# A new order table, and planned times from a replay of five queues, in a FAVOR attention and softplus MLP kernel

## The chip, the cores and the metric

The kernel runs on one core of one Trainium2 chip. The metric is the device time of one execution in microseconds (us). Work is spread over TensorE (PE, matrix products), VectorE (DVE), ScalarE (ACT), GpSimd (POOL) and the DMA queue that SyncE (SP) issues. Each engine takes its own instructions strictly in the order in which the program emitted them; between engines there are only semaphores.

## The reference

```python
q, k, v: (8, 8, 576, 64)      omega: (128, 64)
def phi(x):                    # x scaled by 64 ** -0.25
    h = x @ omega.T - sum(x * x) / 2
    return exp(h - max(h)) / sqrt(128)
kv, z = phi(k).T @ v, sum(phi(k))
attn  = (phi(q) @ kv) / (phi(q) @ z + 1e-6)
x = attn as 4608 tokens x 512
h = x @ w_in                   # 512 -> 2048
g = max(h, 0) + log1p(exp(-abs(h)))
out = g @ w_out                # 2048 -> 512
```

All is float32. The kernel gets near it by splitting operands into a high part in TensorE's fast fp32r form and a low remainder, and by three products (high-high, high-low, low-high) where the reference has one.

## The kernel before, in words

**Tiling.** The 64 heads of 576 rows form 16 quads of four heads (names such as `_4_1_`: batch 4, second quad), each cut into units of 128 rows (`_5_0_2` is unit 2). Keys come first: `xk` is loaded, squared (L594) and summed (L599), split into `spk` high (a cast, L623) and low (a subtraction, L627), projected to `ppk` (L609 in the first batches, L634 later), added up (L647), reduced to a maximum (L651, L659), and exponentiated on ScalarE (L656); `s` sums features (L844, L847), `kt` and `kvs` hold the product with v. Queries go the same way, are multiplied with z for the denominator (`den`, L1006, a multiply with an accumulated sum), inverted (L1011), divided (L1015), turned (`flip`, L1040), written to DRAM and read back as `qq` (L1047, L1063), and multiplied with `kvs` into `xp` (L1096), which is split into `xh` and `xl` (L1110, L1116). In batch 0 the queries skip that turn: `nuq` (L935) is divided on VectorE into `xq` (L939 to L943) and turned by TensorE into `xfq` (L951).

**The MLP** takes tokens in blocks: two of 256 (worked on in turns), then 512 each; `h_5_2` is block 5, feature chunk 2 of 16. Twelve matmuls give `h` (L1167 to L1169), three ScalarE passes and one on VectorE give `u` (L1182), its cast is `gh` (L1186) and the remainder `gl` (L1190), and 12 matmuls add to `acc` (L1227 to L1229), copied out as `o` (L1239, L1244). The last two blocks (tokens from 3584 and 4096) share chunks in pairs: a Strassen-like scheme of seven products `pa`, `pb`, `pc` (L1501) on sums of weights (`tf`, L1423 to L1443, split into `t` and `wi`) and of tokens, collected by VectorE as `ha`, `hb`, `hc` (L1530 to L1539). In it, the fourth product goes into the bank `pb` that the seventh used, so it starts once `hc` (L1534) has read that bank.

**What sets the order.** A step is a `Work`: the engines that may do it with a cost each, what it comes `after`, the buffers that it takes and gives. The table `ORDER` lists every work once, as twice its number plus the choice of its engine. `in_order` (L341) goes through the table, gives each work the buffer that has been free longest by its planned time, and plans its start and end; nothing but the table and these buffers decides what is emitted, and engines follow the emission. `with_fill` (L376) then looks at the planned ends on TensorE and, where a planned gap is long enough, emits `fill` matmuls (L1683) that multiply the identity and whose result is not used. VectorE and GpSimd share an access to SBUF; the plan lets one of them have it at a time for works marked `port`, and in the planned times it goes to the works in the table's order.

The lines that decide this:

```python
e = list(w.on)[k % 2]
t = max([clock.get(e, 0.0)] + [x.end + x.delay for x in w.after])
shared = e == "POOL" or e == "DVE" and w.port
t = max(t, port if shared else 0.0)
n = int((t - last - (0.05 if t < 16 else 0.25)) / (0.43 if t < SLOW else 0.224))
```

Of the kernel before, what the change touches and what calls it, by code (L numbers as in the profile page):

```python
# [19 lines left out]
P = 128  # L20
S = 576
D = 64
M = 128
# [12 lines left out]
SLOW = 7.2  # L36
# [1754 lines left out]
```

## Time and profile before

| | |
|---|---|
| median of 3 runs | 1008.64 us (1008.28 to 1010.65) |
| the profiled execution | 1010.17 us, of which the span is 1008.2 us |
| TensorE busy (matmul) | 985.2 us, 98% |
| VectorE busy | 828.0 us, 82% |
| ScalarE busy | 711.8 us, 71% |
| GpSimd busy | 281.8 us, 28% |
| mean DMA rate | 113 GB/s, 340 and 405 GB/s in the first two of 40 slices |

The span runs from the first to the last instruction of the program; the time of the execution has 1.97 us more around it. A busy share is a mean over stages: a stage in which TensorE has idle time is limited by something else, and the engine that is busy nearly all of that stage is the first to look at.

### The profile page before, as it was taken

To read this page: it belongs to the slowest core of one execution; us is meant where nothing else is said; L and a number is where in the kernel's file an instruction comes from. 1 tells how busy PE (TensorE), PEld (TensorE's weight loads), DVE (VectorE), ACT (ScalarE), POOL (GpSimd) and SP (SyncE) were. 2 spreads that over 40 slices of the span, in tenths; PEclk is the share of its full clock that TensorE was granted. 3 is DMA by queue.
4 is the path that set the end of the run, shared out by engine and by line. 5 is a ranking of instruction groups with operands and counts; after the bars stand their busy time and mean duration, and the time that the engine had idled before them with its cause. 6 is when DMAs were issued, how large, how long until landed. Compare 5 with 4: busy or idle time off the path is not lost. (4 is left out here: it accounts for less than half of the span.)

```text
span 1008.2 us, 17087 instructions
## 1 busy us (share of the span) xinstructions
PE 985.2 (98%) x5563; PEld 809.0 (80%) x5563; DVE 828.0 (82%) x2147; ACT 711.8 (71%) x1735; POOL 281.8 (28%) x251
## 2 busy tenths in 40 slices
PE   8989999999999999999999999999999999999998
PEld 7878888788888888887778887877878778778886
DVE  6999988888888888878889988888888847998710
ACT  5999976668777786878687787878667635675700
POOL 2344432243334331325123441234122012121100
PEclk9999999999999999999999999999999999999999
DMA  9944644423452523441524333352422331000002
GB/s 340 405 144 139 203 128 129 136 76 100 128 153 85 160 80 123 142 131 56 151 83 128 98 118 108 108 148 89 125 95 80 103 96 43 1 1 1 1 11 73
DMA packets 64769, 113.82 MB, mean 113 GB/s; under 512 B 18316, under 2 KB 37672, under 8 KB 64680
## 3 DMA queue, kind: packets, MB, share of 16 engines
q1 hardware_dynamic: 64520, 112.60, 35.2%
q8 instruction: 44, 0.72, 0.3%
q14 instruction: 45, 0.37, 0.1%
q10 hardware_dynamic: 160, 0.13, 0.0%
HBM read 85.68 MB, written 27.03 MB: 112 GB/s over the span
## 5 line engine op out<-in xcount | busy, mean ns | idle before, releaser
L1227 PE MATMUL acc<-wo,gh 128*128 128x512 f32 x512 | 204.0, 398 | 1.6 <-ACT o L1244 1.2
L1228 PE MATMUL acc<-wo,gh 128*128 128x512 f32 x512 | 200.5, 392 | 0.0
L1229 PE MATMUL acc<-wo,gl 128*128 128x512 f32 x512 | 199.5, 390 | 0.0
L1167 PE MATMUL h<-xh,wi 128*128 128x512 f32 (+1 forms) x512 | 189.8, 371 | 2.4 <-DVE u L1182 2.2
L1168 PE MATMUL h<-xl,wi 128*128 128x512 f32 (+1 forms) x512 | 186.7, 365 | 0.3 <-DVE xl L968 0.3
L1169 PE MATMUL h<-xh,wi 128*128 128x512 f32 (+1 forms) x512 | 186.0, 363 | 0.0
L1190 POOL TENSOR_TENSOR gl<-u,gh 128x512 fp32r<-128x512 f32 (+1 forms) x71 | 86.2, 1214 | 227.3 <-ACT gh L1186 111.7
L1227 PEld LDWEIGHTS acc<-wo,gh 128*128 128x128 f32 x512 | 96.3, 188 | 26.2 <-issue 5.0
L1167 PEld LDWEIGHTS h<-xh,wi 128*128 128x128 f32 x512 | 96.7, 189 | 24.4 <-DVE u L1182 6.0
L1229 PEld LDWEIGHTS acc<-wo,gl 128*128 128x128 f32 x512 | 96.2, 188 | 20.9
L1169 PEld LDWEIGHTS h<-xh,wi 128*128 128x128 f32 x512 | 96.7, 189 | 15.7
L1228 PEld LDWEIGHTS acc<-wo,gh 128*128 128x128 f32 x512 | 96.5, 188 | 15.8
L1168 PEld LDWEIGHTS h<-xl,wi 128*128 128x128 f32 x512 | 96.8, 189 | 13.9 <-DVE xl L968 0.5
L1173 ACT ACTIVATE u<-h 128x512 f32<-128x512 f32 (+1 forms) x128 | 69.6, 544 | 46.9 <-PE h L1169 38.9
L1006 DVE CUSTOM_DVE_ANT_0 junk<-phq,zb 128x128 bf16<-128x128 f32 (+1 forms) x228 | 82.8, 363 | 10.8 <-ACT spk L623 0.2
L1182 DVE SCALAR_TENSOR_TENSOR u<-h,u 128x512 f32<-128x512 f32 (+1 forms) x128 | 78.2, 613 | 11.8 <-ACT u L1179 11.4
L1179 ACT ACTIVATE u<-u 128x512 f32<-128x512 f32 (+1 forms) x128 | 74.0, 579 | 2.5
L1176 ACT ACTIVATE u<-u 128x512 f32<-128x512 f32 (+1 forms) x128 | 73.8, 578 | 2.7
L656 ACT ACTIVATE phk<-phk,smk 128x128 f32<-128x128 f32 x208 | 67.0, 394 | 5.7 <-DVE smk L671 5.6
L656 ACT ACTIVATE phq<-phq,smq 128x128 f32<-128x128 f32 x194 | 61.3, 393 | 10.6 <-DVE smq L671 10.6
L1015 POOL TENSOR_TENSOR phq<-phq,dnq 128x512 f32<-128x512 f32 (+1 forms) x34 | 37.7, 1117 | 82.4 <-DVE dnq L1011 49.3
L1186 ACT CAST gh<-u 128x512 fp32r<-128x512 f32 (+1 forms) x83 | 45.6, 552 | 12.6 <-PE acc L1228 6.5
(220 smaller groups left out, 2004.2 us busy)
## 6 DMA issues: line engine op xcount, KB each, us to landing
xk<-kx SPq DMA_DIRECT2D x28, 512.0 KB, 3.5
xq<-qx SPq DMA_DIRECT2D x28, 512.0 KB, 3.5
fdq<-flq SPq DMA_DIRECT2D x28, 512.0 KB, 2.6
qq<-fdq SPq DMA_DIRECT2D x112, 128.0 KB, 3.5
rawi<-wi SPq DMA_DIRECT2D x16, 512.0 KB, 8.5
rawo<-wo SPq DMA_DIRECT2D x16, 512.0 KB, 9.9
out<-o SPq DMA_DIRECT2D x32, 256.0 KB, 3.5
v<-vv SPq DMA_DIRECT2D x14, 576.0 KB
```

The costliest lines, as they stand in the source:

```text
L656: nc.scalar.activation(x, x, AF.Exp, bias=b["sm"][:, 2, c : c + 1])
L1006: nc.vector.tensor_tensor_reduce(jk[r, c % jk.shape[1]], ph[r, c], q.zb[r, h], 1.0, 1e-6, ALU.mult, ALU.add, dn[r, 0, c : c + 1])
L1167: nc.tensor.matmul(b["h"], wh, xh[:, cc, t], start=cc == 0, stop=False)
L1168: nc.tensor.matmul(b["h"], wh, xl[:, cc, t], start=False, stop=False)
L1169: nc.tensor.matmul(b["h"], wl, xh[:, cc, t], start=False, stop=cc == NCC - 1)
L1176: nc.scalar.activation(b["u"], b["u"], AF.Exp, scale=-1.0)
L1179: nc.scalar.activation(b["u"], b["u"], AF.Ln, bias=1.0)
L1182: nc.vector.scalar_tensor_tensor(b["u"], b["h"], 0.0, b["u"], ALU.max, ALU.add)
L1190: (nc.vector if e == "DVE" else nc.gpsimd).tensor_tensor(b["gl"], b["u"], b["gh"].bitcast(F32), ALU.subtract)
L1227: nc.tensor.matmul(dst, gh, w2[fc][:, 0, c], start=start, stop=False, **kw)
L1228: nc.tensor.matmul(dst, gh, w2[fc][:, 1, c], start=False, stop=False, **kw)
L1229: nc.tensor.matmul(dst, gl, w2[fc][:, 0, c], start=False, stop=stop, **kw)
```

## The change

`ORDER` is replaced as a whole: the same works in another order, and for some of them the other engine. By engines, the program has 4837 instructions on TensorE before and 4832 after (the fills: 30 and 25, the five of the very start among them), 2149 and 2143 on VectorE, 1739 and 1712 on ScalarE, 256 and 289 on GpSimd, 453 and 453 on SyncE. GpSimd takes over low parts of `spq` (8), divisions (5), squares of `xq` (5), `gl` (4), `g` (4) and sums `s` (6) among others; VectorE gains 8 casts `gh`, 7 casts `spk` and 11 copies of `phk` and `phq` that ScalarE had, and gives up what went to GpSimd.

The planner gets a second pass, `timed`, which replays five queues: each engine's works in their order, the one that can start first going next, and the shared access going to whichever engine asks for it first. Its times replace those of `in_order` ahead of `with_fill`. Costs and delays in the plan change, and `plan_x` makes its two high parts ahead of its two low parts. Line numbers in the code past the table are 50 higher after than before.

```diff
-SLOW = 7.2
+SLOW = 7.9
+LULL, LULLED = 20.7, 0.9
 ORDER = (
-    384, 394, 386, 410, 434, 456, 415, 418, 440, 462, 437, 390, 392, 396, 398, 416, 400, 402, 478, 500, 522, 544, 388,
...
+    618, 542, 580, 560, 620, 562, 582, 656, 584, 586, 432, 598, 600, 654, 476, 690, 11, 60, 602, 604, 50, 622, 606,
...
-        self.delay = delay or (0.23 if "PE" in on else 0.19)
+        self.delay = delay or (0.21 if "PE" in on else 0.19 if "POOL" in on else 0.14)
...
         if shared:
-            port = w.end
+            port = w.end - (0.13 if e == "POOL" else 0.07)
...
+def timed(out, held):
+    queues = {e: [w for w in out if w.engine == e] for e in ("ACT", "DVE", "PE", "POOL", "SP")}
+    clock, head, ready, done = {e: START.get(e, 0.0) for e in queues}, dict.fromkeys(queues, 0), {}, set()
+    ports, mode, lull = {"DVE": -1.0, "POOL": -1.0}, None, LULLED
+    while len(done) < len(out):
+        best = None
+        for e, q in queues.items():
+            if head[e] == len(q):
+                continue
+            w = q[head[e]]
+            if e not in ready:
+                before = w.after + w.needs + (w.co.needs if w.co else [])
+                if any(id(x) not in done for x in before):
+                    continue
+                ready[e] = max([clock[e]] + [x.end + x.delay for x in before])
+            t = max(ready[e], ports["DVE"] if e == "POOL" else ports["POOL"] if e == "DVE" and w.port else 0.0)
+            if best is None or t < best[0] - 1e-9:
+                best = t, e, w
...
+        w.end = clock[e] = t + w.cost
+        if e == "POOL" or e == "DVE" and w.port:
+            ports[e] = w.end - (0.13 if e == "POOL" else 0.07)
...
-            "SP", dma(P * 4 * cols) + (0.7 if apart and q.qd else 0), load, behind=prev.get("load"),
+            "SP", dma(P * 4 * cols) + (1.6 if early and kind == "k" and u == 1 and not q.qd else 0), load, behind=prev.get("load"),
...
-                "DVE", 0.415 if u < 4 else 0.63, lambda c=c: den(c), after=es + [q.zc] if d is None else [d], behind=d,
+                "DVE", 0.34 if u < 4 else 0.64, lambda c=c: den(c), after=es + [q.zc] if d is None else [d], behind=d,
...
-            "DVE", dve(n * M), flip, after=done, give=[(bu, "phs")], take=[("flip", b, "vs")], port=True,
+            "DVE", dve(n * M), flip, after=done, give=[(bu, "phs")], take=[("flip", b, "vs")],
...
-            h = l = None
+            l = None
             for p in range(2):
-                h = do(
+                hs.append(do(
                     ("DVE", "ACT"), (dve(m) + extra, act(m, PSUM) + extra), lambda e, p=p: x_high(e, p),
-                    after=[a] + old_reads(t0, m), behind=h,
-                )
+                    after=[a] + old_reads(t0, m), behind=hs[-1] if hs else None,
+                ))
+            for p in range(2):
                 l = do(
-                    "DVE", dve(m), lambda p=p: x_low(p), after=[h], behind=l if one else None,
+                    "DVE", dve(m), lambda p=p: x_low(p), after=hs if one else [hs[p]], behind=l if one else None,
...
-        for w in with_fill(*in_order(works, room), room["any"], 1e9, fill):
+        out_, held = in_order(works, room)
+        timed(out_, held)
+        for w in with_fill(out_, held, room["any"], 1e9, fill):
```

**Place A, TensorE, the first queries of batch 0** (the two quads `0_0` and `0_1`; `nuq` numerators, `xfq` turns, `ppq` projections, `h_0_0` the first chunk of the MLP). Before:

```order
L935 MATMUL nuq_0_1_0_609<-kvs_0_1_563,xq_0_1_0_184 128x65 x4
L935 MATMUL nuq_0_1_1_617<-kvs_0_1_563,xq_0_1_1_273 128x65 x4
L935 MATMUL nuq_0_0_2_624<-kvs_0_0_461,xq_0_0_2_277 128x65 x4
L951 MATMUL xfq_0_1_0_630<-ident_72,xq_0_1_0_184 128x128 x2
L951 MATMUL xfq_0_1_1_641<-ident_72,xq_0_1_1_273 128x128 x2
L609 MATMUL ppq_0_1_3_0_648<-omf_82,xq_0_1_3_324 128x128
L609 MATMUL ppq_0_1_3_1_649<-omf_82,xq_0_1_3_324 128x128
```

After:

```order
L985 MATMUL nuq_0_1_0_605<-kvs_0_1_585,xq_0_1_0_209 128x65 x4
L985 MATMUL nuq_0_1_1_612<-kvs_0_1_585,xq_0_1_1_273 128x65 x4
L659 MATMUL ppq_0_1_3_0_620<-omf_82,xq_0_1_3_320 128x128
L659 MATMUL ppq_0_1_3_1_621<-omf_82,xq_0_1_3_320 128x128
L659 MATMUL ppq_0_1_3_0_620<-omf_82,xq_0_1_3_320 128x128
L659 MATMUL ppq_0_1_3_1_621<-omf_82,xq_0_1_3_320 128x128
L1001 MATMUL xfq_0_1_0_628<-ident_72,xq_0_1_0_209 128x128 x2
L1217 MATMUL h_0_0_645<-xh_79,wi0_312 128x256
```

`xfq_0_1_0` and `xfq_0_1_1` stood right behind the numerators; now the projections of unit 3 stand ahead of the first of them, and six matmuls of `h_0_0` and a numerator stand between the two.

**Place B, VectorE, where block 5 of the MLP begins** (`den` rows carry `junk`; their second rows read the sum; `o_4_1` is a copy of block 4's output; `u_5_0` frees the bank that `h_5_2` takes on TensorE). Before, the last rows ahead of `u_5_0`:

```order
L1006 ISA junk_78,dnq_5_0_0_1_6273<-phq_5_0_0_0_6143,zb_5_0_6228 128x128
L1006 ISA dnq_5_0_0_1_6273 128x1
L1006 ISA junk_78,dnq_5_0_0_0_6252<-phq_5_0_0_0_6143,zb_5_0_6228 128x128
L1006 ISA dnq_5_0_0_0_6252 128x1
L1011 RECIPROCAL dnq_5_0_0_1_6273<-dnq_5_0_0_1_6273 128x4
L671 SCALAR_TENSOR_TENSOR smk_5_1_0_5988<-smk_5_1_0_5988 128x8
L1239 COPY o_4_1_6296<-acc_4_1_5133 128x256
L1182 SCALAR_TENSOR_TENSOR u_5_0_6319<-h_5_0_6111,u_5_0_6319 128x512
```

After:

```order
L673 CAST spq_5_0_2_6268<-xq_5_0_2_6245 64x512
L1289 COPY o_4_0_6281<-acc_4_0_5117 128x256
L1056 ISA junk_78,dnq_5_0_0_1_6243<-phq_5_0_0_0_6104,zb_5_0_6218 128x128
L1056 ISA dnq_5_0_0_1_6243 128x1
L1056 ISA junk_78,dnq_5_0_0_1_6243<-phq_5_0_0_0_6104,zb_5_0_6218 128x128
L1056 ISA dnq_5_0_0_1_6243 128x1
L677 TENSOR_TENSOR spq_5_0_2_6268<-xq_5_0_2_6245,spq_5_0_2_6268 64x512 x2
L1232 SCALAR_TENSOR_TENSOR u_5_0_6311<-h_5_0_6198,u_5_0_6311 128x512
```

Three of the eight `den` pairs now come behind `u_5_0`, and the cast and the two low parts of `spq_5_0_2`, whose low parts GpSimd did before, come ahead of it. On TensorE, three matmuls of `acc_4_3` now stand between `h_5_1` and `h_5_2`, where nothing stood before.

**Place C, VectorE, chunk pair 4 of the last two blocks** (`tf` are sums of weights for pair 5). Before:

```order
L1530 TENSOR_TENSOR hb_4_10269<-pb_4_10248,ha_4_10235 128x512
L1308 SCALAR_TENSOR_TENSOR u_3584_7_10277<-hb_3_10127,u_3584_7_10277 128x512
L1428 TENSOR_TENSOR tf0_5_10263<-wi11_1508 128x256
L1429 TENSOR_TENSOR tf0_5_10263<-tf0_5_10263,tf1_5_10264 128x256
L1442 TENSOR_TENSOR tf2_5_10265<-wi10_1245,tf0_5_10263 128x256
L1443 TENSOR_TENSOR tf2_5_10265<-tf2_5_10265,wi10_1245 128x256
L1534 TENSOR_TENSOR hc_4_10294<-pb_4_10248,ha_4_10235 128x512
L1535 TENSOR_TENSOR hc_4_10294<-pc_4_10241,hc_4_10294 128x512
```

After:

```order
L1580 TENSOR_TENSOR hb_4_10265<-pb_4_10252,ha_4_10229 128x512
L1371 TENSOR_TENSOR g_4096_7_10242<-u_4096_7_10161,g_4096_7_10242 128x512
L1358 SCALAR_TENSOR_TENSOR u_3584_7_10240<-hb_3_10122,u_3584_7_10240 128x512
L1478 TENSOR_TENSOR tf0_5_10246<-wi11_1516 128x256
L1479 TENSOR_TENSOR tf0_5_10246<-tf0_5_10246,tf1_5_10247 128x256
L1584 TENSOR_TENSOR hc_4_10286<-pb_4_10252,ha_4_10229 128x512
L1585 TENSOR_TENSOR hc_4_10286<-pc_4_10208,hc_4_10286 128x512
L1492 TENSOR_TENSOR tf2_5_10248<-wi10_1254,tf0_5_10246 128x256
L1493 TENSOR_TENSOR tf2_5_10248<-tf2_5_10248,wi10_1254 128x256
```

The two `tf2_5` rows have gone behind both `hc_4` rows, and one `g` row has come in ahead of `u_3584_7`. For pair 2 the same rows stand as before, but the `u_4096_3` row that stood between `hb_2` and `hc_2` now stands ahead of `hb_2`.

## Rows read from the trace of the kernel before

**Rows 1.** The page: busy time of each engine, share of the span, instructions.

```profile
PE 985.2 (98%) x5563; PEld 809.0 (80%) x5563; DVE 828.0 (82%) x2147; ACT 711.8 (71%) x1735; POOL 281.8 (28%) x251
```

**Rows 2.** Windows: start:end, length, busy us by engine, granted clock, DMA share, GB/s.

```profile
0.00:50.00 50.00, 44.68 (x348) 39.54 (x349) 40.28 (x141) 37.52 (x110) 15.19 (x23) 0.97 0.98 373
50.00:125.00 75.00, 70.35 (x578) 59.40 (x578) 73.36 (x196) 71.11 (x193) 32.81 (x28) 1.00 0.50 161
125.00:475.00 350.00, 349.98 (x2015) 288.18 (x2015) 297.71 (x815) 261.84 (x663) 114.63 (x102) 1.00 0.39 118
475.00:525.00 50.00, 46.65 (x255) 36.80 (x254) 44.04 (x115) 36.42 (x89) 14.63 (x13) 1.00 0.36 107
525.00:850.00 325.00, 322.32 (x1700) 260.51 (x1699) 272.79 (x706) 231.51 (x548) 86.87 (x71) 1.00 0.35 105
850.00:925.00 75.00, 72.50 (x321) 59.24 (x320) 69.45 (x126) 47.63 (x91) 13.54 (x12) 1.00 0.01 4
36.00:44.00 8.00, 5.79 (x52) 4.96 (x50) 7.90 (x25) 6.18 (x17) 2.65 (x4) 1.00 1.03 409
45.00:48.00 3.00, 3.00 (x16) 2.55 (x15) 2.97 (x13) 2.48 (x8) 1.03 (x1) 0.50 1.03 410
```

**Rows 3.** Timeline at the start, TensorE and GpSimd: start, length, [idle before <-releaser].

```profile
12.30 2.88 PE L1683 MATMUL fill<-ident 128*128 128x128 f32 x16
...
12.58 0.61 POOL L594 TENSOR_TENSOR xk<-xk 128x256 f32<-128x256 f32 x1 [0.37 <-DMA xk<-k]
```

**Rows 4.** Timeline of TensorE at the first queries of batch 0.

```profile
42.75 0.41 PE L951 MATMUL xfq<-ident,xq 128*128 128x128 f32 x2 [0.77 <-DVE dnq L939]
43.49 0.41 PE L951 MATMUL xfq<-ident,xq 128*128 128x128 f32 x2 [0.33 <-DVE xq L943]
```

**Rows 5.** Timeline of SyncE's issues and TensorE at 478 to 486 us.

```profile
478.54 2.64 SPq L1063 DMA_DIRECT2D qq<-fdq  x4
...
485.18 1.08 PE L1096 MATMUL xp<-qq,kvs 128*64 128x256 f32 x8 [1.12 <-DMA qq<-fdq]
```

**Rows 6.** Timeline of GpSimd, VectorE and TensorE where block 5 begins.

```profile
513.76 2.73 POOL L627 TENSOR_TENSOR spq<-xq,spq 64x512 fp32r<-64x512 f32 x2 [4.99 <-ACT spq L623]
...
515.31 1.32 DVE L1006 CUSTOM_DVE_ANT_0 junk<-phq,zb 128x128 bf16<-128x128 f32 x1
516.57 0.08 DVE L1006 DVE_READ_ACCUMULATOR2_ANT dnq<- 128x1 f32 x1
516.68 0.29 DVE L1006 CUSTOM_DVE_ANT_0 junk<-phq,zb 128x128 bf16<-128x128 f32 x1
...
518.77 0.50 PE L1167 MATMUL h<-xh,wi 128*128 128x512 f32 x1 [1.01 <-DVE u L1182]
```

**Rows 7.** Timeline of VectorE, GpSimd and TensorE in chunk pairs 2 and 4.

```profile
871.81 0.68 DVE L1308 SCALAR_TENSOR_TENSOR u<-h,u 128x512 f32<-128x512 f32 x1
...
873.32 1.46 DVE L1442 TENSOR_TENSOR tf<-wi,tf 128x256 f32<-128x256 f32 x1
...
873.22 1.28 POOL L1321 TENSOR_TENSOR g<-u,g 128x512 fp32r<-128x512 f32 x1 [3.01 <-ACT g L1316]
...
875.89 0.50 PE L1501 MATMUL pb<-xh,t 128*128 128x512 f32 x1 [1.62 <-DVE hc L1534]
...
901.45 0.43 DVE L1442 TENSOR_TENSOR tf<-wi,tf 128x256 f32<-128x256 f32 x1
901.91 1.41 DVE L1443 TENSOR_TENSOR tf<-tf,wi 128x256 f32<-128x256 f32 x1
...
903.97 0.50 PE L1501 MATMUL pb<-xh,t 128*128 128x512 f32 x1 [0.60 <-DVE hc L1534]
```

**Rows 8.** Groups by line and shape: count, busy us, mean ns, idle before.

```profile
L1190 POOL TENSOR_TENSOR gl<-u,gh 128x512 fp32r<-128x512 f32 x50 | 66.2, 1324 | 174.7 <-ACT gh L1186 74.5 <-DVE gh L1186 51.1 <-DVE dnq L1011 15.1
...
L1006 DVE CUSTOM_DVE_ANT_0 junk<-phq,zb 128x128 bf16<-128x128 f32 x224 | 81.7, 365 | 10.7 <-ACT spk L623 0.2
...
L1190 DVE TENSOR_TENSOR gl<-u,gh 128x512 fp32r<-128x512 f32 x46 | 33.3, 726 | 2.8 <-ACT gh L1186 1.8
...
L1186 DVE CAST gh<-u 128x512 fp32r<-128x512 f32 x38 | 17.9, 471 | 2.5 <-PE acc L1228 0.7
```

More of the change, by code (lines that the diff above doesn't have):

```diff
@@ L319, with __init__ @@
 class Work:
-    def __init__(self, on, emit, after=(), take=(), give=(), delay=None, spare=0, behind=None, port=False, mode=None):
+    def __init__(self, on, emit, after=(), take=(), give=(), delay=None, spare=0, behind=None, port=False, mode=None, co=None):
         self.on, self.emit, self.port = on, emit, port
@@ L328, in __init__ @@
         self.take, self.give, self.spare = take, give, spare
-        self.delay = delay or (0.23 if "PE" in on else 0.19)
+        self.delay = delay or (0.21 if "PE" in on else 0.19 if "POOL" in on else 0.14)
         self.end, self.behind, self.engine = None, behind, None
         self.mode, self.cost = mode, 0.0
+        self.co, self.freed, self.needs = co, 0.0, []
 def change(old, new):
@@ L343, in in_order @@
     clock, held = dict(START), {}
-    free = {n: 0.0 for names in room.values() for n in names}
-    port, mode, out = 0.0, None, []
+    free = {n: (0.0, None) for names in room.values() for n in names}
+    port, mode, lull, out = 0.0, None, LULLED, []
     for k in ORDER:
@@ L353, in in_order @@
             assert len(names) > w.spare
-            box[key] = n = min(names, key=free.get)
-            t = max(t, free.pop(n))
+            box[key] = n = min(names, key=lambda n: free[n][0])
+            at, giver = free.pop(n)
+            w.freed = max(w.freed, at)
+            w.needs += [giver] if giver else []
             held.setdefault(n, []).append([t, 1e9, len(out), 1e9])
+        t = max(t, w.freed, w.co.freed if w.co else 0.0)
         shared = e == "POOL" or e == "DVE" and w.port
@@ L362, in in_order @@
         w.cost *= 2 if e == "PE" and t < SLOW else 1
+        if e == "SP" and t >= LULL:
+            w.cost, lull = w.cost + lull, 0.0
         w.end = clock[e] = t + w.cost
@@ L366, in in_order @@
         if shared:
-            port = w.end
+            port = w.end - (0.13 if e == "POOL" else 0.07)
         for box, key in w.give:
-            free[box[key]] = w.end + w.delay
+            free[box[key]] = w.end + w.delay, w
             held[box[key]][-1][1::2] = w.end + w.delay, len(out)
@@ L373, in in_order @@
     return out, held
+def timed(out, held):
[16 more added lines that the diff above has]
+                best = t, e, w
+            elif e == "POOL" and best[1] == "DVE" and t < best[0] + 1e-6 and best[2].port and ready[e] <= ready["DVE"] + 0.02:
+                best = t, e, w
+        t, e, w = best
+        w.cost = w.on[e]
+        if e == "PE":
+            w.cost += change(mode, w.mode)
+            w.cost *= 2 if t < SLOW else 1
+            mode = w.mode
+        elif e == "SP" and t >= LULL:
+            w.cost, lull = w.cost + lull, 0.0
+        w.end = clock[e] = t + w.cost
+        if e == "POOL" or e == "DVE" and w.port:
+            ports[e] = w.end - (0.13 if e == "POOL" else 0.07)
+        del ready[e]
+        head[e] += 1
+        done.add(id(w))
+    for spans in held.values():
+        for x in spans:
+            x[0] = out[x[2]].end - out[x[2]].cost
+            if x[3] < 1e9:
+                x[1] = out[x[3]].end + out[x[3]].delay
 def with_fill(out, held, banks, until, emit):
@@ L719, in plan_unit @@
                     ("ACT", "DVE"), (act(w) + 0.1, dve(w, 2) + 0.115), lambda e, j=j: high(e, j), after=[ld], behind=hs[-1] if hs else None,
-                    take=[] if j else [("sp", b, "sps")], port=True,
+                    take=[] if j else [("sp", b, "sps")], port=True, co=hs[0] if j else None,
                 )
@@ L1019, in plan_queries @@
             d = do(
-                "DVE", 0.415 if u < 4 else 0.63, lambda c=c: den(c), after=es + [q.zc] if d is None else [d], behind=d,
+                "DVE", 0.34 if u < 4 else 0.64, lambda c=c: den(c), after=es + [q.zc] if d is None else [d], behind=d,
                 take=[] if c else [("dn", b, "dns")], give=[(q.slots, "zb")] if u == NU - 1 and c == n - 1 else [], port=True,
             )
-            d.delay = 0.0 if c < n - 1 else d.delay
+            d.delay = 0.11 if c < n - 1 else d.delay
         d = do("DVE", 0.09, invert, after=[d])
@@ L1133, in pieces_of @@
                 x_lows[t0, m, 2 * q.qd + p] = l
-                hs.append(h)
         if one and q.n + 1 < len(quads):
```

506 rows, old and new, of the table ORDER are left out of this document.

## The prediction

> **What bounds the kernel now.** I read the page's busy line first: TensorE is busy for 985.2 us of the span of 1008.2, VectorE for 828.0, ScalarE for 711.8, GpSimd for 281.8 [rows 1]. The change adds and removes no product, so nearly all that it can save is TensorE's 23.0 us without work, and the next question is where they lie. The windows tell it: 5.3 us before 50 us, 4.7 between 50 and 125, almost none up to 475, 3.4 in the 50 us after that, 2.7 from 525 to 850, 2.5 from 850 to 925, and the rest at the end, where the last copies leave [rows 2]. The same rows say what limits each: before 50 us the DMA engines (share 0.98); between 50 and 125 us VectorE, busy 73.36 of 75 us, with ScalarE close behind (71.11); from 125 us on TensorE itself, but for single waits. I then looked each wait up in the timelines: the row of the first TensorE instruction behind it names its length and its releaser, and the releaser's own rows show what held that up. The sum below is a sum over such waits, and each term has its place.
>
> **The start.** Eight fills stand in one place at 12.30 us (16 records, 2.88 us, so 0.36 each), and the projection of the next unit follows them at once; but GpSimd had begun to square that unit, on landed data, at 12.58 [rows 3]. So these fills covered no wait: they made one. After, four stand there, which is 1.4 us less. The projections feed VectorE, which waits for them here. But the loads run at nearly full share, and whether work that starts earlier still finds its data is not in these rows: between 0 and -1.4 I take the middle, -0.8, rounded up for the cover that four fills may still be.
>
> **Place A.** Two turns wait for VectorE's division, 0.77 and 0.33 us [rows 4]; projections and half of `h_0_0` now stand in front of them, so they cost nothing if VectorE comes no later. It may, since it is busy 7.90 of the 8 us before 44 us. TensorE is busy only 5.79 of those 8, and right after them, from 45 to 48 us, its granted clock is 0.50, which is 1.2 of 2.4 GHz; at the full clock its 3.00 us of work there would have been 1.5 [rows 2]. With fewer holes ahead of it the drop may go or may come elsewhere. Together that is 0 to -2.6; I take -1.0, the two waits without their last tenth, and nothing for the clock, because behind it VectorE is the limit and takes most of what TensorE gains.
>
> **From 50 to 125 us.** VectorE limits, and the rows of the program give it neither less nor more work that matters: some casts come, some low parts go. A cast is 471 ns, a low part 726 [rows 8]; a handful either way is -2 to +2. I take 0.
>
> **xp_4_1_2048.** SyncE issues the four reads of `qq` from 478.54 on for 2.64 us, and TensorE waits 1.12 us for the last of them [rows 5]. After, the write ahead of them goes before a load that it followed, and TensorE's order has other work between the last issue and this product. -1.1, between 0 and -1.12.
>
> **Place B.** Three pairs of `den` rows go behind `u_5_0`, 0.29 + 0.08 us each, 1.1 in all. GpSimd's low parts of `spq_5_0_2` (2.73 us for two) go too, and with them the row that they stretched from 0.29 to 1.32 [rows 6]: another 1.0. In come a cast and two low parts on VectorE, by the nearest rows 0.47 + 2 x 0.73 = 1.9 [rows 8]. That alone makes `u_5_0` 0.2 us earlier. What decides is TensorE: three matmuls of `acc_4_3` stand ahead of `h_5_2` now; between 525 and 850 us a matmul of any size takes 0.19 us in the mean (322.32 / 1700 [rows 2]) and these are of the widest, so some 0.7 us, an estimate. 0.2 + 0.7 nearly covers the wait of 1.01 [rows 6]: -0.9. If GpSimd is again beside the remaining `den` rows, one of them costs 1.03 more and half of the wait stays.
>
> **Place C.** The fourth product waits for `hc`, 1.62 us in pair 2 and 0.60 in pair 4 [rows 7]. In pair 4, 0.43 + 1.41 us of `tf` rows leave the way and a `g` row of about 0.7 enters: `hc` is 1.1 us sooner and the 0.60 goes. In pair 2 one `u` row of 0.68 leaves, so at least 0.6 of the 1.62 goes; the 1.0 left is the `tf` row of 1.46 beside GpSimd's `g` row, which goes only if GpSimd comes at another time. -1.2, between 0 and -2.2. The three fills planned there remain, behind the same wait.
>
> **The rest.** What is left of the idle time after 475 us and before 850 is 3.35 - 1.12 - 1.01 + 2.68 = 3.9 us in waits of at most about a microsecond, each at some place where two engines' orders meet by accident. A new order meets elsewhere. I take a fifth off, -0.8 (0 to -3.9), and put against it new waits: a third of what terms B, C, xp and this one remove (4.0), rounded up, +1.4, and at most all of it. I take the third because the long stretch from 125 to 475 us, made in the same way, has none to speak of.
>
> **The sum.** -0.8 - 1.0 + 0 - 1.1 - 0.9 - 1.2 - 0.8 + 1.4 = -4.4 us. The profiled execution took 1010.17 us (span 1008.2 and 1.97 around it); that is 1.53 above the median of the runs, 1008.64. So 1005.8 on the profiled execution's scale, and 1004.2 on the median's. All bounds at their good ends give -14, at their bad ends +6.
>
> What costs nothing: new planned times alone move no instruction; they only choose the number of fills. That the plan no longer counts the flip as sharing SBUF is of that kind: the instruction is the same, and it stands behind the same division as before.
>
> **The rivals.**
>
> *No change.* The 1.8 us at the start and place A are swallowed by VectorE between 50 and 125 us, and new waits are as many as those that go after 475 us but for about one: -1.1, so 1007.5. For it speaks VectorE's 73.36 of 75; against it, that four waits of 0.6 to 1.6 us late in the run have named causes, each of which the order takes away.
>
> *Larger gain.* The clock's drop goes as well and is not swallowed (-1.5), pair 2 loses its whole wait (-1.0), half of the other late waits go (-1.1 more): -8, so 1000.6. For it: in places B and C a row stretched beside GpSimd stands right ahead of the wait, and in B the GpSimd instructions beside it are gone. Against it: VectorE's load up to 125 us, and that only these places are known to lose their neighbour.
>
> *Slower: GpSimd stretches VectorE.* GpSimd gets 33 more instructions, of 1.3 us like `gl` (1324 ns [rows 8]), and a VectorE row beside one can grow by 1.03 us (1.32 - 0.29, 1.46 - 0.43 [rows 6, 7]). In the program's rows, up to the first chunk of block 3, GpSimd has 101 before and 100 after, so the stretch from 50 to 125 us is spared; of the rest, nine more stand where TensorE waits for VectorE (10 and now 14 from `h_4_14` to `h_5_4`, 16 and now 21 from `hb_2` on). If all nine hit a row on the way to a product, that is 9.3 us; four hits outweigh the 4.4 us of the sum. With half of them (4.7), the gains of start and place A kept (-1.8) and the new waits (+1.4), the others gone: 1008.6 + 4.3 = 1012.9. Against it: the `den` rows, most often hit, are 365 ns in the mean and 290 with nothing beside them [rows 6, 8], 16.8 us over 224 rows, which is 0.07 us for each of the 251 GpSimd instructions by that line; and what GpSimd takes over, VectorE mostly gives up (0.73 us for a low part). The Trainium skill ("SBUF - State Buffer", "Who interferes with whom") has the rule behind it: a VectorE instruction with two SBUF inputs and a GpSimd instruction that reads SBUF exclude one another for the whole of the instruction, and the order of issue decides who blocks. The rows of 1.32 and 1.46 beside GpSimd agree. By that rule more GpSimd instructions are a risk wherever VectorE asks second, which is this rival; it changes no other term.
>
> **How the numbers follow.** The forecast has 0.45 with a range of its own from 1002 to 1006.5; the larger gain 0.22; no change 0.22; slower 0.11. A measurement of this kernel tells 0.3% from nothing, 3.0 us: faster is below 1005.6, slower above 1011.7. The forecast lies four times in five below 1005.6, so faster is 0.36 + 0.22 = 0.58, the same 0.09 + 0.22 = 0.31, slower 0.11. The range reaches to both sides until a tenth is left on each: 999.0 to 1010.5.
>
> **What would show it.** Start: the projection that came at 15.24 comes near 14. Place A: no wait at the two turns, and a granted clock of 1.00 at 45 to 48 us or the same drop elsewhere. xp, place B: no wait of TensorE over 0.3 us at the products named. Place C: `pb` waits for `hc` about 1 us in pair 2, not at all in pair 4. The windows: TensorE's idle time falls from 23.0 to about 18.5, most of the difference after 475 us. I am wrong if VectorE's busy time grows by over 5 us, if 50 to 125 us holds more idle time of TensorE than 4.7, or if the waits that go come back under other names within the same 50 us.

## The result, and the profile after

The changed kernel takes 994.47 us, the median of 4 runs (992.61 to 1000.24), against 1009.0 of the kernel before (4 runs, 1008.28 to 1010.65): ratio 0.9863 [0.9818, 0.9908], 14.5 us less. The sign was forecast; the time lies below the whole range. The profiled execution took 996.06 us, with a span of 994.2.

The page's busy line, to be held against [rows 1]:

```profile
PE 982.4 (99%) x5553; PEld 808.9 (81%) x5553; DVE 799.1 (80%) x2141; ACT 703.8 (71%) x1708; POOL 314.5 (32%) x284
```

TensorE's work is almost the same (2.8 us less), so of the 14.0 us that the span lost, 11.2 are time without work: 23.0 us before, 11.8 now. And VectorE is busy for 28.9 us less with six instructions fewer, although 33 works more on GpSimd could have stretched its rows.

The windows of the kernel after, in the columns of [rows 2]:

```profile
0.00:50.00 50.00, 45.84 (x347) 39.55 (x348) 38.59 (x141) 38.28 (x111) 15.80 (x26) 1.00 0.97 370
50.00:125.00 75.00, 73.18 (x599) 62.84 (x600) 71.97 (x204) 73.17 (x204) 28.54 (x26) 1.00 0.50 165
125.00:475.00 350.00, 349.65 (x2004) 287.58 (x2003) 294.03 (x819) 263.94 (x658) 126.33 (x110) 1.00 0.39 119
475.00:525.00 50.00, 49.67 (x276) 40.42 (x275) 42.27 (x116) 36.93 (x90) 16.47 (x14) 1.00 0.41 125
525.00:850.00 325.00, 324.21 (x1710) 263.60 (x1710) 265.52 (x707) 222.40 (x520) 103.98 (x88) 1.00 0.33 101
850.00:925.00 75.00, 74.42 (x329) 60.55 (x328) 68.89 (x128) 51.20 (x98) 18.18 (x17) 1.00 0.00 1
36.00:44.00 8.00, 7.31 (x67) 6.27 (x67) 7.76 (x29) 8.00 (x23) 1.63 (x2) 1.00 1.03 409
45.00:48.00 3.00, 2.47 (x21) 1.98 (x21) 2.57 (x12) 3.00 (x10) 1.65 (x2) 1.00 1.02 407
```

Length less TensorE's busy time is the idle time of a stretch: from 5.32 to 4.16 before 50 us, from 4.65 to 1.82 up to 125, from 3.35 to 0.33 in 475 to 525, from 2.68 to 0.79 up to 850, from 2.50 to 0.58 up to 925. The three late stretches together went from 8.53 to 1.70. From 45 to 48 us the granted clock is 1.00 where it was 0.50. That the order did this is not shown: of the seven profiles with the old start (the kernel before and six experiments) four have a stretch at half clock between 43 and 59 us and three have none, and of the seven with the new start two have one before 50 us.

The longest waits of TensorE after, by the view of waits (us in total, times, longest):

```profile
PE fill L1733 <- DVE marks L488: 1.1, 1, 1.1
PE ppk L659 <- DMA xk<-k: 0.9, 2, 0.6
PE nuq L985 <- ACT kvs L875: 0.6, 1, 0.6
PE ppk L684 <- DVE spk L677: 0.6, 1, 0.6
PE h L1217 <- DVE u L1232: 0.5, 1, 0.5
```

The first two belong to the very start and to the loads. No single wait of more than 0.65 us is left that another engine's order makes. The 0.64 at `nuq` is new: it stands at place A, ahead of the turns.

The places of the prediction, in TensorE's timeline after: the start, place A, `xp_4_1_2048`, place B, place C (pair 2, then pair 4):

```profile
12.46 2.07 PE L1733 MATMUL fill<-ident 128*128 128x128 f32 x8
14.60 1.29 PE L659 MATMUL ppk<-omf,xk 64*128 64x128 f32 x8
18.27 2.00 PE L869 MATMUL kt<-xk 128*128 128x65 f32 x16
...
44.68 0.39 PE L1001 MATMUL xfq<-ident,xq 128*128 128x128 f32 x2
...
478.56 1.08 PE L1146 MATMUL xp<-qq,kvs 128*64 128x256 f32 x8
...
510.66 0.39 PE L1279 MATMUL acc<-wo,gl 128*128 128x512 f32 x1
510.89 0.39 PE L1217 MATMUL h<-xh,wi 128*128 128x512 f32 x1
...
861.85 0.83 PE L1733 MATMUL fill<-ident 128*128 128x128 f32 x6
862.79 0.50 PE L1551 MATMUL pb<-xh,t 128*128 128x512 f32 x1
...
890.62 0.39 PE L1551 MATMUL pb<-xh,t 128*128 128x512 f32 x1
```

No row has a bracket: the waits of [rows 4 to 7] are gone. In pair 2 the view hides a part, though. Six fill records of 0.83 us stand in front of the product, as they did before, and they count as work. Experiments below that have no fills there show what they cover. The new order, in the run without planned fills:

```profile
855.06 1.65 PE L1551 MATMUL pb<-x,t 128*128 128x512 f32 x6 [0.33 <-DVE hb L1580]
857.49 0.51 PE L1551 MATMUL pb<-xh,t 128*128 128x512 f32 x1 [0.79 <-DVE hc L1584]
```

The old order, in the run with the new start alone:

```profile
864.75 1.66 PE L1565 MATMUL pb<-x,t 128*128 128x512 f32 x6 [0.98 <-DVE hb L1594]
868.70 0.80 PE L1565 MATMUL pb<-xh,t 128*128 128x512 f32 x1 [2.29 <-DVE hc L1598]
```

So in pair 2 TensorE lacks 1.12 us of useful work where it lacked 3.27. What GpSimd and VectorE do there in the kernel after:

```profile
857.45 1.34 POOL L1371 TENSOR_TENSOR g<-u,g 128x512 fp32r<-128x512 f32 x1 [0.19 <-ACT g L1366]
862.59 1.30 POOL L1371 TENSOR_TENSOR g<-u,g 128x512 fp32r<-128x512 f32 x1 [3.80 <-ACT g L1366]
```

```profile
857.57 1.51 DVE L1474 TENSOR_TENSOR tf<-wi,wi 128x256 f32<-128x256 f32 x1
...
860.96 0.43 DVE L1492 TENSOR_TENSOR tf<-wi,tf 128x256 f32<-128x256 f32 x1
861.42 0.43 DVE L1493 TENSOR_TENSOR tf<-tf,wi 128x256 f32<-128x256 f32 x1
862.04 0.69 DVE L1584 TENSOR_TENSOR hc<-pb,ha 128x512 f32<-128x512 f32 x1 [0.19 <-PE pb L1551]
```

The same two `tf2` rows still stand ahead of `hc`, but of GpSimd's two `g` rows only the first now stretches a VectorE row ahead of `hc`: it runs beside an earlier sum, as it did before (1.51 us both times). The second, at 862.59, comes behind the `tf2` rows. The row that took 1.46 us in [rows 7] takes 0.43. VectorE even waits 0.19 us for TensorE.

The groups after, against [rows 8]:

```profile
L1056 DVE CUSTOM_DVE_ANT_0 junk<-phq,zb 128x128 bf16<-128x128 f32 x224 | 68.8, 307 | 11.0
L1240 POOL TENSOR_TENSOR gl<-u,gh 128x512 fp32r<-128x512 f32 x56 | 74.1, 1323 | 106.6 <-ACT gh L1236 43.6 <-DVE gh L1236 31.0 <-PE acc L1279 13.8
```

The 224 `den` rows fell from 365 ns to 307, 12.9 us in all, while GpSimd's `gl` grew from 50 to 56. Summing, over VectorE's rows, what each takes beyond the 15th percentile of its own form gives a stretch of 72.0 us before and 48.6 after; VectorE rows stretched by over 0.35 us are 75 before and 47 after, and every one of them has a GpSimd instruction beside it. GpSimd has more instructions and meets fewer.

### The profile page after: what moved, and what is told of

Its sections match the earlier page's. It is cut to its first block, busy times and chain, and to the rows that moved or that the text cites. A ratio compares the mean times of both kernels' runs of the same rounds, so it can differ in the third digit from the quotient of the medians.

```text
span 994.2 us, 17161 instructions
## 1 busy us (share of the span) xinstructions
PE 982.4 (99%) x5553; PEld 808.9 (81%) x5553; DVE 799.1 (80%) x2141; ACT 703.8 (71%) x1708; POOL 314.5 (32%) x284
## 4 chain that ended last, share of the span: by engine, by line
PE 83%; DVE 7%; ACT 5%; DMA 3%; issue 1%; SPq 0%; POOL 0%; DVEq 0%; ACTq 0%; POOLq 0%
PE acc L1277 12%; PE acc L1278 12%; PE acc L1279 12%; PE h L1217 10%; PE h L1218 9%; PE h L1219 9%; PE xp L1146 3%; PE kt L824 3%; PE pb L1551 2%; PE ppk L684 2%; PE ppq L684 2%; PE pa L1551 1%; DMA xq<-q 1%; PE pc L1551 1%; PE h L1393 1%
## 5 line engine op out<-in xcount | busy, mean ns | idle before, releaser
L1240 POOL TENSOR_TENSOR gl<-u,gh 128x512 fp32r<-128x512 f32 (+1 forms) x74 | 89.0, 1203 | 148.2 <-ACT gh L1236 58.4
L1218 PEld LDWEIGHTS h<-xl,wi 128*128 128x128 f32 x512 | 96.7, 189 | 14.1 <-DVE xl L1018 0.5
L1065 POOL TENSOR_TENSOR phq<-phq,dnq 128x512 f32<-128x512 f32 x39 | 41.4, 1067 | 135.5 <-DVE dnq L1061 129.6
L1056 DVE CUSTOM_DVE_ANT_0 junk<-phq,zb 128x128 bf16<-128x128 f32 (+1 forms) x228 | 70.6, 310 | 11.2
L1226 ACT ACTIVATE u<-u 128x512 f32<-128x512 f32 (+1 forms) x128 | 75.7, 592 | 2.7
L1229 ACT ACTIVATE u<-u 128x512 f32<-128x512 f32 (+1 forms) x128 | 75.1, 590 | 2.9
L677 POOL TENSOR_TENSOR spq<-xq,spq 64x512 fp32r<-64x512 f32 (+1 forms) x29 | 37.8, 1304 | 97.7 <-ACT spq L673 78.5
```

Source lines behind the costliest of these rows:

```text
L1218: nc.tensor.matmul(b["h"], wh, xl[:, cc, t], start=False, stop=False)
L1226: nc.scalar.activation(b["u"], b["u"], AF.Exp, scale=-1.0)
L1229: nc.scalar.activation(b["u"], b["u"], AF.Ln, bias=1.0)
L1240: (nc.vector if e == "DVE" else nc.gpsimd).tensor_tensor(b["gl"], b["u"], b["gh"].bitcast(F32), ALU.subtract)
```

## The experiments

Ratios are to the kernel before on the same chip, with their 95% intervals. "Old" and "new" are the tables before and after.

**The fills.** Are the 20 fills placed by the plan worth anything?

```diff
-            if names and n > 0:
+            if False:
```

> The changed kernel without any fill but the five of the very start (20 fills fewer, some 0.3 us of TensorE each). Theory (the order and the choice of engines make the gain, fills do not): ratio to the kernel before 0.984 to 0.990, as the changed kernel's 0.986. Rival (the fewer fills, and the clock that they keep, are the gain): TensorE's clock falls to half somewhere before 50 us and 2 to 5 us of the gain are gone, ratio 0.988 to 0.991 or more.

994.19 us, 0.9865 [0.9841, 0.9888]: the same as with them. So what the replay chooses as fills is not where the gain is; what is left is the order, the choice of engines, and the buffers that the plan gives by its times.

**Order and engines apart.** The first kernel has the new order, but gives the 334 works their old engines behind the planner; the second has the old order and the new engines.

```diff
-        for w in with_fill(out_, held, room["any"], 1e9, fill):
+        planned = with_fill(out_, held, room["any"], 1e9, fill)
+        for i in SWAPPED:
+            w = works[i]
+            w.engine = [e for e in w.on if e != w.engine][0]
+        for w in planned:
```

> The changed kernel's places in the order, buffers and fills, but each of the 334 works whose engine differs gets the engine that it had before. Theory (places and engines were fitted to each other, so that VectorE and GpSimd meet less; VectorE's busy time fell from 828.0 to 799.1 us): most of the gain goes, ratio 0.993 to 1.005, VectorE busy over 815 us. Rival A (TensorE's work was put in front of its waits, and that alone is the gain): ratio 0.985 to 0.991. Rival B (VectorE has less work of its own by the choice of engines, places don't matter): all the gain goes, 0.998 to 1.002.

> The kernel before, with its places, buffers and fills, but each of the 334 works gets the engine that it has after. Theory (fitted to each other): no gain or a loss, ratio 0.998 to 1.012, VectorE's den rows stretched as before (mean 350 ns or more). Rival A (places alone): no gain, 0.998 to 1.002. Rival B (VectorE's load by the choice of engines alone): ratio 0.986 to 0.992, VectorE busy near 800 us.

1038.72 us, 1.0312 [1.0288, 1.0335], and 1054.93 us, 1.0458 [1.0434, 1.0481]. Both are far slower than either whole, and slower than any of the theories had it (at most 1.005 and 1.012). The largest waits of TensorE in the first:

```profile
PE h L1240 <- DVE u L1255: 5.7, 8, 1.2
PE acc L1302 <- DVE gl L1263: 3.9, 4, 1.9
```

and in the second:

```profile
PE h L1190 <- DVE u L1205: 8.6, 13, 2.0
PE ppq L657 <- DVE phq L670: 5.5, 7, 2.3
```

All are waits for VectorE. By the measure above its stretch is 72.3 us in the first, that of the kernel before, and 89.4 in the second: the new engines in old places stretch more, in their own places far less. The first is 30 us slower than the kernel before with the same stretch, so the sum of the stretch alone does not set the time. The gain cannot be split into a share of the order and a share of the engines.

**How tight the fit is.** After, with 33 of the 334 works, every tenth, on their old engine (same edit, shorter list).

> The changed kernel, but every tenth of the 334 works whose engine differs (33, spread over the run) gets the engine of before; all 334 cost 44 us over the changed kernel. If each misfit has a price of its own: a tenth, 4 to 5 us, ratio 0.990 to 0.992. If there is slack that takes the first ones in: ratio 0.986 to 0.988. If a few set off a chain: over 0.995.

1000.34 us, 0.9923 [0.9904, 0.9943], by the medians 5.9 more than after: 0.18 us for each work. New waits stand together, by TensorE's timeline:

```profile
675.79 0.50 PE L1223 MATMUL h<-xh,wi 128*128 128x512 f32 x1 [1.13 <-DVE u L1238]
...
684.39 0.51 PE L690 MATMUL ppq<-omr,spq 128*128 128x256 f32 x2 [0.43 <-DVE phq L703]
685.27 0.47 PE L690 MATMUL ppq<-omr,spq 128*128 128x256 f32 x2 [0.38 <-DVE phq L703]
```

**Where the gain is, by time.** New table for the first 410 works (to about 58 us), and for the first 1400 (to about 215 us), then old, both under the new planner; and the old for the first 1400, then new, under the old planner. Fills are kept to the first 58, 60 and 100 us.

```diff
-        for w in with_fill(out_, held, room["any"], 1e9, fill):
+        for w in with_fill(out_, held, room["any"], 58.0, fill):
```

> The new order up to its 410th work only (some 58 us: fills, place A and the first chunk of the MLP), then the rest in the order of before; the kernel with the new order up to 215 us had ratio 0.994 (5.7 us). If what is gained in the start is passed on (my terms start and place A, 1.8 us, and the clock, 1.5): ratio 0.9965 to 0.998. If VectorE swallows it between 50 and 125 us, as I took for the clock: 0.999 to 1.001, and the 5.7 us come from the order after 58 us. If the start alone makes it all: below 0.9955.

> The new order up to its 1400th work (chunk 6 of block 2, some 215 us), then all that is left in the order of before; fills only up to 60 us, as in the changed kernel there. If the gain comes in two halves as the two traces have it (TensorE reaches block 2 about 4.5 us sooner, the other 9 us come after 470 us), this keeps the first: ratio 0.994 to 0.997, some 4.5 us, and the waits at xp_4_1_2048, h_5_2 and pb of the kernel before are back at their places. If what is gained early is taken back by waits later (a fixed rate of the later stages), ratio 0.998 to 1.000.

> The mirror of the run that went from the new order to the old: the old order up to its 1400th work (block 2, some 215 us), then all that is left in the new order, the fills of the start as before. If the two parts add up, this gains what that run left of the whole: ratio 0.990 to 0.994 (the whole 0.986, the first part alone 0.994), the waits from 475 us on gone. If the second part needs the first (queues that stand differently at the seam), ratio above 0.995.

1004.52 us, 0.9959 [0.9943, 0.9974]; 1003.36, 0.9943 [0.9929, 0.9957]; and 1004.75, 0.996 [0.9948, 0.9972]. So 4.1 us come from the start, 1.6 more from 58 to 215 us (the two intervals overlap), and the new order behind that gives 3.8 by itself. In the profile of the new start alone, TensorE's work stands 4.5 us earlier than before at `h_0_0`, and 4.7 at 470 us. The first part and the second give 9.5 of the 14.5 us. Behind its seam, at 257, 324 and 808 us, the kernel that begins old has waits that the kernel after has not (1.19, 0.63 and 0.66 us, 2.5 of the 5.0 that are missing): the parts are fitted to one another too. With the new order up to 215 us, the late waits were back, in pair 2 without the fills that covered a part of them:

```profile
PE pb L1565 <- DVE hc L1598: 2.9, 2, 2.3
...
PE h L1231 <- DVE u L1246: 1.5, 2, 1.0
PE acc L1291 <- ACT o L1308: 1.2, 1, 1.2
```

These runs also tell the table from the planner. Behind 58 us the new start alone is the old table under the new planner: TensorE's idle time from 475 to 925 us is 8.1 us, 8.5 before. The kernel that begins old is the new table under the old planner there, and has 3.3. The late waits went by the table.

**The moves of the prediction, alone.** In the kernel before, five moves are to take away the late waits that I priced and one more, by order only; fills past 100 us are left out as well: `xp` behind six products of `acc`; `u_5_0` ahead of two `den` pairs; a copy of `acc_6_2` ahead of `den` pairs; the `tf2` rows behind `hc` in pairs 2 and 4. The last two, as works of the table:

```diff
-  9008, 9016, 8958,   ...   8960, 8859,
+  9008, 8958,         ...   8960, 9016, 8859,
-  9204, 9212, 9154,   ...   9156, 9079,
+  9204, 9154,         ...   9156, 9212, 9079,
```

> The kernel before with five moves in its order and no change of engines: xp_4_1_2048 behind six products of acc_4 (wait before 1.12 us), u_5_0 ahead of the last two den pairs (1.01), the copy of block 6's acc out to o ahead of five den pairs (1.18), the tf2 rows behind hc in pairs 2 and 4 (1.62 and 0.60): 5.5 us of waits; no fills past 100 us. Theory 1 (waits are places, each can be taken away for itself): all five waits under 0.3 us and 4.5 to 5.5 us gained, ratio 0.9945 to 0.9955. Theory 2 (as I forecast: a third comes back as new waits): 3.5 us, ratio 0.996 to 0.997. Theory 3 (the stage's rate is fixed, waits come back under other names): ratio 0.998 to 1.000.

1007.29 us (12 runs), 0.9991 [0.9979, 1.0002]: of 5.5 us of waits 1.2 were gained by the medians, at most 2.1 and perhaps nothing. From TensorE's timeline:

```profile
491.85 0.74 PE L648 MATMUL ppk<-omr,spk 128*128 128x256 f32 x4 [1.52 <-ACT s L809]
...
869.20 1.66 PE L1515 MATMUL pb<-x,t 128*128 128x512 f32 x6 [0.98 <-DVE hb L1544]
871.65 0.50 PE L1515 MATMUL pb<-xh,t 128*128 128x512 f32 x1 [0.79 <-DVE hc L1548]
```

`xp`, `u_5_0` and pair 4 wait no more, and the copy's wait fell from 1.18 to 0.70. A product a little behind `xp` waits 1.52 us, 0.40 before: that wait was handed on. In pair 2 the move did work: held against the old order without late fills (0.98 and 2.29) it took 1.5 us away, and the 0.98 is no new wait, it had stood under a fill. Nor is the whole 1.12 at `xp` owed to its place: with the old order there it is 0.31 us in the kernel that is new up to 215 us, and 0.36 with the six engines below. The profiled execution, the fastest of the twelve (1006.25 us), is 3.9 us below that of before. So that these moves gave little is shown by the medians; that a wait goes to the next product, at one place only.

**Taking the neighbour away.** Also in the kernel before: six GpSimd works that run beside stretched VectorE rows ahead of waits go to VectorE, in the same places (the edit of the engine swaps, six works). This gives VectorE more to do.

> The kernel before, order as it was, but six GpSimd works that run beside a stretched VectorE row just ahead of a wait go to VectorE: both low parts of spq_5_0_2, gl_7_1 and a sum of s_7_1, g_4096_3, gl_3584_7. If the stretch by the shared access is what makes these waits: u_5_0's wait 1.01 -> 0.7 or less, the copy's 1.18 -> 0.6 or less, hc's in pair 2 1.62 -> 0.6, in pair 4 0.60 -> 0; 2 to 3 us in all, ratio 0.997 to 0.998, although VectorE has six instructions more. If VectorE's load makes them: the waits stay or grow, ratio 1.000 to 1.002.

1005.14 us, 0.9963 [0.9951, 0.9975]: 3.4 us less than before, by six works.

```profile
871.15 0.42 DVE L1447 TENSOR_TENSOR tf<-wi,tf 128x256 f32<-128x256 f32 x1
872.70 0.50 PE L1506 MATMUL pb<-xh,t 128*128 128x512 f32 x1 [0.58 <-DVE hc L1539]
```

The `tf` row of 1.46 us takes 0.42, and pair 2's wait falls by 1.04, the stretch of that row. The waits of pair 4 and at the copy went altogether, place B's fell only from 1.01 to 0.78. VectorE's busy time is 827.1 us for 2153 instructions, 828.0 for 2147 before: the stretch saved pays for all six.

**The same on a large scale, with a control.** In the kernel before, 56 GpSimd works beside which a VectorE row is stretched by over 0.5 us go to VectorE; the control moves 55 works that have no such row beside them, mostly of the same kinds (2 low parts of `spq` where the first has 11, 12 of `spk` where it has 3).

> The kernel before, order and fills as they were, but the 56 GpSimd works beside which a VectorE row was stretched by over 0.5 us in its trace (47 us of stretch in all) are done by VectorE. If being stretched at the wrong place is what costs (theory): VectorE takes 56 rows of 0.4 to 0.7 us for 47 us less stretch, its busy time falls by 5 to 15 us, and the time by 3 to 8 us, ratio 0.992 to 0.997. If the load on VectorE costs (rival): 56 rows more on it make it slower, ratio 1.002 to 1.015.

> The control to the kernel above: the kernel before with 55 other GpSimd works given to VectorE, of the same kinds and each next to one of those 56 in GpSimd's queue, but with no stretched row beside them. Theory: as much load and no stretch saved, VectorE busy over 850 us, slower, ratio 1.005 to 1.03. Rival (load does not matter, GpSimd being emptier is what helps): as fast as the kernel above.

1007.19 us, 0.9983 [0.9969, 0.9998], and 1029.9 us, 1.0232 [1.0207, 1.0257]. The busy line of the first page:

```profile
PE 984.8 (98%) x5563; PEld 810.5 (81%) x5563; DVE 824.6 (82%) x2206; ACT 710.2 (71%) x1735; POOL 206.3 (21%) x192
```

and of the control's:

```profile
PE 990.6 (96%) x5563; PEld 807.8 (79%) x5563; DVE 858.8 (84%) x2205; ACT 712.7 (69%) x1735; POOL 216.3 (21%) x193
```

The counts on each engine differ by one; VectorE's busy time differs by 34.2 us and the time by 22.7. So meetings on the shared access cost time, and count for as much as load: 55 works more on VectorE cost 21.4 us, and the meetings that 56 works made give that back and 1.3 more. But they give little beyond it, less than the theory had (0.992 to 0.997): 38 us of stretch were saved (72.0 to 33.6), but the 59 rows that VectorE took over cost nearly as much, so that its busy time fell by 3.4 us, and waits came back elsewhere, such as these:

```profile
490.24 0.51 PE L641 MATMUL ppk<-omr,spk 128*128 128x256 f32 x2 [1.58 <-ACT s L802]
491.86 0.79 PE L641 MATMUL ppk<-omr,spk 128*128 128x256 f32 x2 [1.11 <-DVE xl L1123]
```

**What is left in the new kernel.** After, with the 19 GpSimd works beside which a row is stretched by over 0.7 us on VectorE.

> The changed kernel with the same treatment: its 19 GpSimd works with over 0.7 us of stretch beside them (17.5 us in all) go to VectorE. Theory: TensorE waits little there by now, so little can come of it, ratio 0.983 to 0.990 (the changed kernel 0.986). Rival (the order was fitted with these places, each change of it costs as the 33 did, 0.18 us each): 3 to 4 us slower than the changed kernel, 0.989 to 0.991.

993.98 us, 0.9861 [0.984, 0.9881], the same as after. The stretch fell from 48.6 to 32.7 us for 20 rows more on VectorE, and the time did not move: the meetings that are left are worth no more than those rows.

## Why the prediction was wrong, step by step

**Right:** `xp` (1.12 to 0, though four other profiles of the old order have at most 0.4 there), place B (1.01 to 0), pair 4 (0.60 to 0), and that most of the idle time would go after 475 us. At place A both turns stopped waiting, but 0.64 us came in at the numerators. Taking nothing for the clock was right, too. The kernel with the five moves has the old start and no drop: a matmul of `h` that starts at 48.39 us in the kernel before starts at 47.59 there, but a later one at 69.79 against 69.60, so what the full clock gained was gone again by then, as was said. A stretched row ahead of a wait as its cause is shown by the six swapped engines in pairs 2 and 4 (1.04 and 0.60 us); at place B it was 0.23 of the 1.01.

**Right by luck: the start.** `kt` is 0.65 us earlier in the two profiles, -0.8 said. But TensorE's pace there changed at 14.1 us in the one and 16.7 in the other (last section). In the run with 33 engines set back, whose start is the new one and whose pace changes at 13.8 us, `kt` is 1.9 us earlier than before and `h_0_0` 2.6, where start and place A had 1.8 in the sum.

**Wrong first: "The rest" took a fifth, 0.8 us, off the other late waits, and pair 2 kept 1.0.** By these and by xp, B and C, the idle time after 475 us should have fallen by 2.6 (1.1 + 0.9 + 1.2 + 0.8 - 1.4); it fell by 6.8. Of the 4.2 between, 3.4 are the other late waits, 4.2 us in all, which went nearly whole, and 1.0 is pair 2. The new waits came to about what was priced: all that the view of waits shows behind 475 us are five, 1.5 us together, the longest 0.64. But of what went that is under a fifth, not the third they were priced by. I had called the late waits accidental meetings, of which a new order misses a share. In its place the runs show that they go with the new table, under either planner, and that places and engines in it are fitted together, so tightly that a tenth of the engines set back costs 5.9 us. Five moves in the old order, by contrast, gave 1.2 of 5.5 us. The diff shows which of the two the change is: all but 226 of the 4905 works have another place in the table, by six places in the median.

**Wrong second: "From 50 to 125 us" at 0.** The idle time there fell from 4.65 to 1.82. I read 73.36 busy us of 75 as work that VectorE must do, and counted only what came and went. But stretch is counted as busy: by the measure above it was 9.9 us in that stage and is 4.5, and VectorE is now busy for 71.97 us with eight rows more, while TensorE does 2.83 us more. Less stretch alone does not give this: with the 56 works moved it is 5.2 us there, and TensorE's idle time still 3.97. Nor does the new start alone (3.61 idle); with the new order up to 215 us it is 1.69. The rival "No change" had VectorE swallow the gain of the start, too; it was passed on whole, since the start brings VectorE's rows forward with it (the first `u` at 51.48 us in the new start alone, 55.98 before).

**The rival that turned round: GpSimd stretches VectorE.** It priced each new GpSimd instruction by the meetings of the old order. The price of a meeting was right: a row's stretch of about a microsecond, in both traces, and in pair 2 a wait of the same size. The count was not: it depends on who stands beside whom, and the new table sets that anew. The rule of the Trainium skill ("SBUF — State Buffer", "Who interferes with whom") agrees with the rows (0.43 us alone, 1.46 beside GpSimd); I drew only the risk from it. VectorE's 828.0 us against 799.1 is its other side. The larger gain, at 1000.6, had the right mechanism for the late waits, but took only half of the others, and counted the clock's drop, which came to nothing.

**Open.** How the new table was found, no run shows; the old table as a whole under the new planner was not run. How much of the 2.83 us from 50 to 125 us is less stretch and how much better places was not told apart. Why the five moves gave so little by the medians, their one trace does not show. And the start has a part that the runs do not settle, below.

## What to carry to other kernels

Take the idle time of each stage as what a new order may give there, and do not count an engine as full before the stretch in its rows is taken off: compare each form's mean with its shortest rows, and look at what runs beside the long ones. At a wait, look for the stretched row ahead of it and move its neighbour; this costs little and is tested by a swap of engines with a control of equal load. Here a few local moves gave a fraction of their waits, and an order fitted anew with its engines nearly the whole idle time of the late stages, so price the two apart. Before you read a wait as gone, see whether work without use, such as a fill, covers it: run the kernel once without.

## What the runs showed of the hardware

Matmuls at the very start run at half pace (a fill every 0.21 us, later every 0.11), and when they speed up differs from one execution to another. The windows give a granted clock of 1.00 there, but the trace has no record of the clock that early: the first one comes where the pace changes. Four fill records in the kernel after:

```profile
6.16 1.22 PE L1733 MATMUL fill<-ident 128*128 128x128 f32 x4
9.96 1.22 PE L1733 MATMUL fill<-ident 128*128 128x128 f32 x4
```

and in the one with the new start alone:

```profile
5.79 0.71 PE L1747 MATMUL fill<-ident 128*128 128x128 f32 x4
...
15.07 2.00 PE L883 MATMUL kt<-xk 128*128 128x65 f32 x16
```

The first changes to the faster pace only at 16.7 us, the second at 4.8, and `kt` then starts at 15.07 instead of 18.27. The old start changed at 13 us or later in all seven profiles that have it, with `kt` at 18.35 us or later; the new one before 6 us in three of seven, at about 10 in two, at 13.8 and 16.7 in two. Perhaps the new start brings this about, and a part of its 4.1 us is this; against it stands that up to 4.7 us TensorE has the same ten fills and the same first projection in both. That the kernel after measured 992.61 and 992.88, but also 996.06, would fit. The 1000.24 us have another cause at least in part: a mean granted clock of 0.991, where the other three have 0.999 or 1.000. What sets the change of pace, no run here shows.

Fills may hold up the clock. Both kernels with the old order and no late fills have a granted clock of 0.50 for a few microseconds from the last part of pair 2's wait of 2.29 us on (from 868.3 and 864.9 us); no other profile has one there. So their gains, 4.1 and 5.7 us, may be somewhat small for what their part of the new order gives.

The last is a reading of ScalarE's rows. From 40 to 75 us the same ACTIVATE (`xq` from `ppq`, 16 rows) has a mean of 556 ns after and 388 before, and yet it is no slower: a row starts before the one ahead of it has ended, by 0.09 to 0.17 us before and 0.21 to 0.35 after, and from one end to the next it is about 0.26 us in both. The mean of rows that overlap is not their pace. ScalarE is the busiest engine there now, all 25 us from 50 to 75; the time fell all the same.
